# The last stores of a fused retention and hard-swish kernel: who copies the last quarter, and in how many transfers it leaves

## The chip, the cores and the metric

The kernel runs on one core of a Trainium2 chip. The metric is device time in microseconds (us) of one execution, lower is better. Besides plain timings there is one execution under the hardware profiler; its trace and its page are what this document reads.

## The reference

Per batch and head, `ret = ((q k^T) / sqrt(64) * D) v` with the decay mask `D[i, j] = gamma_h^(i-j)` for `i >= j` and zero above. The heads are laid side by side, so that `x` has 4608 rows (8 batches of 576 positions) and 512 columns. Then comes a feed-forward layer:

```python
h = x @ w_in                               # 512 -> 2048
g = h * np.clip(h + 3.0, 0.0, 6.0) / 6.0
out = g @ w_out                            # 2048 -> 512, float32
```

## The kernel before, in words

**Blocks of tokens.** The 576 positions of a batch are cut into 512 "main" positions and 64 "rest" positions. The feed-forward layer works on blocks of 512 tokens (`NMB` is 9). Block `kb` from 0 to 7 holds the main positions of batch `kb`. Block 8, the last, holds the rests of all eight batches: its 512 tokens are eight groups of 64, and 128 neighbouring tokens of it are the rests of two batches.

**Two products per block.** `gemm1` makes the 2048 hidden values (L554 matmuls, L562 on ScalarE, L563 on VectorE). For blocks 2 to 8, `g2_seven` makes the second product by seven half-size products, in the manner of Strassen, instead of eight (`plan`, L738 to L748). Each entry of `plan` is two units, `u = 0` and `u = 1`, of eight matmuls each (L697); `u` is the half of 128 tokens. The output block of 512 tokens by 512 columns is so made in four quarters C11, C12, C21 and C22 of 256 tokens by 256 columns.

**The last block.** There the accumulator named `x` lies in two separate PSUM tiles, which the profile calls `xo` (`u = 0`) and `xtu` (`u = 1`). The last entry of `plan` finishes C21 in them, and nothing is left to do on TensorE after it. `copy_half(u)` (L726 to L729) runs right behind each unit of that entry: it copies one half, 128 tokens by 256 columns, from PSUM to a tile `osh` and calls `store`.

**Where the stores go.** `store` (L594 to L602) and `store_quarter` (L655 to L666) write to the output in DRAM. For a block of rests the 128 tokens of a tile belong to two batches, so that their rows lie in two places of the output, 576 rows apart. Both functions therefore issue two DMA transfers in the last block, one for the first 64 partitions, on the queue of SyncE (SP), and one for the other 64, on the queue of ScalarE (ACT).

**Order.** The order of the instructions on each engine is the order in which the program issues them. A DMA that is issued from ScalarE takes its place in ScalarE's own instruction order, and ScalarE's next copy stands behind it. At the end of the program SP waits for the semaphores of all DMA queues, one after the other (these waits carry the line of the launch, L1067), and then for the other engines.

Of the kernel before, what the change touches and what calls it, by code (L numbers as in the profile page):

```python
# [17 lines left out]
def kernel(  # L18
# [16 lines left out]
    nc = tc.nc  # L35
    B, H, S, D = q.shape
# [4 lines left out]
    HALF = P // 2  # L41
# [4 lines left out]
    MAIN = MBLK  # L46
# [38 lines left out]
    def bank(shape, dtype, name):  # L85
        return psum.tile(shape, dtype, tag="ph", bufs=4, name=name)
# [504 lines left out]
        for fc in range(2):  # L591
            g1_act(kb, banks[fc], fc)

    def store(kb, mc, cols, src):  # L594
        if kb < B:
            r0 = kb * S + P * mc
            nc.sync.dma_start(out[r0:r0 + P, cols], src)
        else:
            for i in range(2):
                r0 = (2 * mc + i) * S + MAIN  # L600
                queue = nc.scalar if i else nc.sync
                queue.dma_start(out[r0:r0 + HALF, cols], src[i * HALF:i * HALF + HALF])  # L602

    pouts = {}

    def g2(kb, mc, part):
        gt = gts[kb]
        if part == 0:
            pouts[kb, mc] = bank([P, DM], FP32, name=f"pout_{kb}_{mc}")
        pout = pouts[kb, mc]  # L610
        for fc in range(4 * part, 4 * part + 4):
            nc.tensor.matmul(pout, gt[:, fc, P * mc:P * mc + P], wout16[:, fc, :],  # L612
                             start=(fc == 0), stop=(fc == NFC - 1))
        if part == 3:
            osb = work.tile([P, DM], FP32, tag="osb", bufs=4, name=f"osb_{kb}_{mc}")
            nc.scalar.copy(osb, pout)
            store(kb, mc, slice(0, DM), osb)

    KH, TH, NH = NFC // 2, MBLK // 2, DM // 2
# [16 lines left out]
    def token_sums(kb, which, c0=0, c1=KH):  # L636

        gt = gts[kb]

        def a(i, j):  # L640
            return gt[:, KH * j + c0:KH * j + c1, TH * i:TH * i + TH]

        def s(name):
            if (kb, name) not in sums:
                sums[kb, name] = work.tile([P, KH, TH], FP16, tag=f"sum_{name}", bufs=1,
                                           name=f"sum_{name}_{kb}")
            return sums[kb, name]

        x, y, op = {"s1": (lambda: a(1, 0), lambda: a(1, 1), ALU.add),
                    "s2": (lambda: s("s1")[:, c0:c1], lambda: a(0, 0), ALU.subtract),  # L650
                    "s3": (lambda: a(0, 0), lambda: a(1, 0), ALU.subtract),
                    "s4": (lambda: a(0, 1), lambda: s("s2")[:, c0:c1], ALU.subtract)}[which]
        nc.vector.tensor_tensor(out=s(which)[:, c0:c1], in0=x(), in1=y(), op=op)  # L653

    def store_quarter(kb, i, j, src):  # L655

        cols = slice(NH * j, NH * j + NH)
        if kb < B:
            r0 = kb * S + TH * i
            nc.sync.dma_start(out[r0:r0 + TH, cols].rearrange("(u p) n -> p u n", u=2), src)  # L660
        else:
            rest = out.rearrange("(m x s) n -> x s m n", x=2, s=S)
            for x in range(2):
                queue = nc.scalar if x else nc.sync
                queue.dma_start(rest[x, MAIN:S, 2 * i:2 * i + 2, cols],
                                src[x * HALF:x * HALF + HALF])  # L666

    def g2_seven(kb, last=False):

        gt = gts[kb]  # L670

        def w(i, j):
            return wout16[:, KH * i:KH * i + KH, NH * j:NH * j + NH]

        def a(i, j):
            return gt[:, KH * j:KH * j + KH, TH * i:TH * i + TH]

        def s(name):
            return sums[kb, name]

        acc = {}

        def get(name):
            if name not in acc:
                if last and name == "x":
                    acc[name] = [psum.tile([P, NH], FP32, tag=t, name=f"x{t}_{kb}")
                                 for t in ("o", "tu")]
                else:
                    whole = bank([P, 2, NH], FP32, name=f"{name}_{kb}")
                    acc[name] = [whole[:, 0], whole[:, 1]]  # L690
                    wholes[name] = whole
            return acc[name]

        def product(name, u, left, right, first):
            dst = get(name)[u]
            for c in range(KH):
                newest[0] = nc.tensor.matmul(  # L697
                    dst, left()[:, c, P * u:P * u + P], right[:, c, :],
                    start=(first and c == 0 and (u == 0 or name not in wholes)),
                    stop=(c == KH - 1), skip_group_check=True)  # L700

        kept, wholes = {}, {}

        def parts(name, tile):
            if name in wholes:
                return [(wholes[name], tile)]
            return [(acc[name][u], tile[:, u]) for u in range(2)]

        def keep(name):
            kept[name] = work.tile([P, 2, NH], FP32, tag="keep_" + {"m5": "m1"}.get(name, name), bufs=1,  # L710
                                   name=f"keep_{name}_{kb}")
            for src, dst in parts({"m5": "z"}.get(name, "x"), kept[name]):
                nc.scalar.copy(dst, src)

        def total(i, j, name, src):
            osb = work.tile([P, 2, NH], FP32, tag="osb", bufs=4, name=f"osb_{kb}_{i}_{j}")
            for (a0, dst), (_, a1) in zip(parts(src, osb), parts(src, kept[name])):
                nc.vector.tensor_tensor(out=dst, in0=a0, in1=a1, op=ALU.add)
            store_quarter(kb, i, j, osb)

        def copy_total():
            osb = work.tile([P, 2, NH], FP32, tag="osb", bufs=4, name=f"osb_{kb}_1_0")
            nc.scalar.copy(osb, wholes["x"])
            store_quarter(kb, 1, 0, osb)

        def copy_half(u):  # L726
            osb = work.tile([P, NH], FP32, tag="osb", bufs=4, name=f"osh_{kb}_{u}")
            nc.scalar.copy(osb, acc["x"][u])
            store(kb, 2 + u, slice(0, NH), osb)  # L729

        def unit(name, u, left, right, first, then=()):
            def do():
                product(name, u, left, right, first)
                for f in then:
                    f()
            return do

        plan = [  # L738
            ("x", lambda: a(0, 0), w(0, 0), True, [lambda: keep("m1")]),
            ("y", lambda: a(0, 1), w(1, 0), True,  # L740
             [lambda: total(0, 0, "m1", "y"), lambda: token_sums(kb, "s3")]),
            ("x", lambda: s("s2"), wts["t2"], False, [lambda: keep("u2")]),
            ("z", lambda: s("s1"), wts["t1"], True,
             [lambda: keep("m5"), lambda: token_sums(kb, "s4")]),
            ("x", lambda: s("s3"), wts["t3"], False, [lambda: total(1, 1, "m5", "x")]),
            ("z", lambda: s("s4"), w(1, 1), False, [lambda: total(0, 1, "u2", "z")]),
            ("x", lambda: a(1, 1), wts["t4"], False, [] if last else [copy_total]),
        ]  # L748
        units = []
        for n, (name, left, right, first, then) in enumerate(plan):  # L750
            for u in range(2):
                after = then if u else []
                if last and n == len(plan) - 1:
                    after = [lambda u=u: copy_half(u)]
                units.append(unit(name, u, left, right, first, after))
        return units
# [315 lines left out]
```

## Time and profile before

| | us |
|---|---|
| median of 3 runs | 294.95 (294.73 to 295.85) |
| the profiled execution's own time | 295.87 |
| its span, first to last instruction | 294.1 |
| outside the span (295.87 - 294.1) | 1.8 |
| TensorE busy in the span | 282.4 (96%) |
| last matmul of C21's second half ends | 289.05 |

The span is what the trace shows; the run's own time is longer than the span by what lies outside it. The profiled execution took 0.9 us more than the median of the plain runs. Times "at 289.49" in the text are us from the start of the span. In lists of groups or of the timeline, a row gives engine, line, operation, the tile written and the tile read. SPq and ACTq are the sequencers of SyncE and ScalarE issuing DMAs. In the list of DMA queues, q1 is the hardware queue that SP issues to, and q10 the one that ScalarE issues to; of each queue come packets, MB, and the packets' time as a share of that of 16 DMA engines over the stretch.

### The profile page before, as it was taken

The page shows a single profiled execution, that of the slowest core. Times are in us where ns is not written, and L with a number is a line of the kernel's source. Part 1 is how long each engine was busy: PE and PEld are TensorE (multiplying, and loading weights), DVE is VectorE, ACT ScalarE, POOL GpSimd, SP SyncE. Part 2 cuts the span into 40 slices and gives each one's busy share as a digit, 9 for nine tenths or more (in the row PEclk, how much of TensorE's full clock was granted, in tenths as well). Part 3 has the DMA queues.
Part 4 walks back from the last instruction along what each step waited for, and adds up shares of the span by engine and source line. Part 5 has one row for each costly group of instructions (what it writes and reads, how often), then busy time and mean ns, then how long its engine had stood idle before and what let it go on. Part 6 is the DMA issues. An engine that isn't in the chain of part 4 may idle for free.

```text
span 294.1 us, 8348 instructions
## 1 busy us (share of the span) xinstructions
PE 282.4 (96%) x3495; PEld 175.5 (60%) x3495; DVE 227.3 (77%) x377; ACT 167.1 (57%) x297; POOL 107.5 (37%) x134
## 2 busy tenths in 40 slices
PE   5999999999999989999999999999999999999993
PEld 1644445644544668458845884588458745874682
DVE  4768656798758996799879987998799588728960
ACT  5567537784358634774477447744774286337711
POOL 8963568359343323333334333455550000000000
PEclk9799999999999999999999999999999999999998
DMA  9999999999999999999999799999992240120014
GB/s 66 148 193 206 189 165 218 161 135 139 127 211 164 152 104 119 168 135 87 120 150 157 79 125 164 128 92 124 151 149 48 74 109 0 38 79 30 0 39 108
DMA packets 156630, 35.68 MB, mean 121 GB/s; under 512 B 143792, under 2 KB 155568, under 8 KB 156592
## 3 DMA queue, kind: packets, MB, share of 16 engines
q0 software_dynamic: 117264, 18.36, 94.7%
q1 hardware_dynamic: 38736, 16.26, 29.5%
q8 instruction: 27, 0.44, 0.7%
q10 hardware_dynamic: 592, 0.52, 0.6%
q14 instruction: 11, 0.09, 0.1%
HBM read 36.70 MB, written 9.44 MB: 157 GB/s over the span
## 4 chain that ended last, share of the span: by engine, by line
PE 86%; DMA 6%; POOL 4%; issue 1%; DVE 1%; ACT 0%; ACTq 0%; POOLq 0%
PE ph L554 39%; PE x L697 14%; PE z L697 9%; PE pout L612 7%; PE y L697 5%; DMA qk<-qv 3%; DMA win<-in_moe_w_in_dram 3%; POOL qv L103 2%; PE o L458 2%; PE sc L425 2%; PE o L479 1%; POOL kn L103 1%; PE ph L577 1%; PE xtu L697 1%; PE xo L697 1%
## 5 line engine op out<-in xcount | busy, mean ns | idle before, releaser
L554 PE MATMUL ph<-xt,win 128*128 128x512 f16 x560 | 122.5, 379 | 0.1
L562 ACT ACTIVATE u<-ph,cb 128x512 f32<-128x512 f32 x144 | 98.4, 688 | 26.0 <-PE ph L554 25.5
L563 DVE SCALAR_TENSOR_TENSOR gt<-u,ph 128x512 f16<-128x512 f32 x144 | 95.7, 683 | 22.4 <-ACT u L562 20.9
L554 PEld LDWEIGHTS <-win 128*128 128x128 f16 x560 | 54.6, 98 | 64.8 <-DMA win<-in_moe_w_in_dram 0.6
L103 POOL DMA_DIRECT2D qv<-in_v_dram x40 | 33.9, 849 | 39.0 <-PE x L697 16.9
L103 POOL DMA_DIRECT2D kn<-in_k_dram x40 | 34.2, 856 | 37.2 <-PE ph L554 12.7
L697 PEld LDWEIGHTS <-sum_s 128*128 128x128 f16 x448 | 42.6, 98 | 6.8 <-issue 1.5
L103 POOL DMA_DIRECT2D qv<-in_q_dram x40 | 33.8, 845 | 31.1 <-PE z L697 9.9
L697 PEld LDWEIGHTS <-gt 128*128 128x128 f16 x336 | 32.1, 98 | 5.5
L612 PE MATMUL pout<-wout,gt 128*128 128x512 f16 x128 | 29.5, 379 | 0.0
L697 PE MATMUL x<-wsum_t,sum_s 128*128 128x256 f16 x192 | 23.1, 273 | 1.2 <-issue 1.2
L531 ACT CAST tm<-th 128x256 f16<-128x256 f32 x24 | 9.7, 405 | 20.4 <-DVE th L526 20.3
L612 PEld LDWEIGHTS <-gt 128*128 128x128 f16 x128 | 11.9, 98 | 13.0
L431 DVE TENSOR_TENSOR at<-sc,mask 128x1024 f16<-128x1024 f32 x14 | 17.0, 1215 | 1.9 <-PE sc L425 1.9
L653 DVE TENSOR_TENSOR sum_s<-gt 128x1024 f16<-128x1024 f16 (+1 forms) x21 | 18.1, 863 | 0.2
L307 DVE TENSOR_TENSOR qv<-qv,gqv 128x1024 f16<-128x1024 f16 x26 | 17.8, 683 | 0.0
L489 ACT CAST xt<-o 128x512 f16<-128x512 f32 x28 | 15.0, 585 | 4.2 <-PE o L479 4.2
L542 DVE TENSOR_TENSOR ta<-u,th 128x256 f32<-128x256 f32 x24 | 10.2, 424 | 6.2 <-ACT th L529 5.2
L697 PE MATMUL z<-wout,sum_s 128*128 128x256 f16 x112 | 14.5, 274 | 0.0
L697 PE MATMUL y<-wout,gt 128*128 128x256 f16 x112 | 14.3, 274 | 0.0
L697 PE MATMUL z<-wsum_t,sum_s 128*128 128x256 f16 x112 | 13.6, 273 | 0.0
L697 PE MATMUL x<-wsum_t,gt 128*128 128x256 f16 x96 | 11.5, 273 | 0.0
(117 smaller groups left out, 256.4 us busy)
## 6 DMA issues: line engine op xcount, KB each, us to landing
out_dram<-osb SPq DMA_DIRECT2D x32, 256.0 KB, 2.5
kn<-in_k_dram POOLq DMA_DIRECT2D x32, 128.0 KB, 6.0
qv<-in_q_dram POOLq DMA_DIRECT2D x32, 128.0 KB, 6.5
qv<-in_v_dram POOLq DMA_DIRECT2D x32, 128.0 KB, 6.1
wout<-in_moe_w_out_dram POOLq DMA_DIRECT2D x4, 512.0 KB, 15.0
win<-in_moe_w_in_dram POOLq DMA_DIRECT2D x3, 512.0 KB, 11.3
win<-in_moe_w_in_dram POOLq DMA_DIRECT2D x2, 256.0 KB, 6.5
kn<-in_k_dram POOLq DMA_DIRECT2D x8, 64.0 KB, 3.6
```

The costliest lines, as they stand in the source:

```text
L103: loaded[c]["dma"].append(nc.gpsimd.dma_start(dst[p0:p0 + n], src[b, :, s0:s0 + n, :].rearrange("h s d -> s h d")))
L307: scaled = nc.vector.tensor_tensor(out=qv, in0=qv, in1=gqv, op=ALU.mult)
L431: nc.vector.tensor_tensor(out=at.rearrange("t a j p s -> t (a j p) s"), in0=sc.rearrange("t a j p s -> t (a j p) s"), in1=mask64[:, None, ...
L489: nc.scalar.copy(xt_at(cs[0], 0, 2 * P).rearrange("e p (j x s) -> e p j x s", j=2, x=2) [:, :, :, half, :], o[half].rearrange("e j p s -> ...
L531: nc.scalar.copy(tm, ta)
L542: nc.vector.tensor_tensor(out=ta, in0=st[c]["u"][1], in1=st[c]["sum"], op=ALU.add)
L554: newest[0] = nc.tensor.matmul(ph, win16[:, dmc, P * fc:P * fc + P], xt_of(kb)[:, dmc, :], start=(dmc == 0), stop=(dmc == NCC - 1))
L562: nc.scalar.activation(u, ph, ACTF.Relu, bias=cb[:, 0:1], scale=1.0 / 6.0)
L563: nc.vector.scalar_tensor_tensor(out=gts[kb][:, fc, :], in0=u, scalar=1.0, in1=ph, op0=ALU.min, op1=ALU.mult)
L612: nc.tensor.matmul(pout, gt[:, fc, P * mc:P * mc + P], wout16[:, fc, :], start=(fc == 0), stop=(fc == NFC - 1))
L653: nc.vector.tensor_tensor(out=s(which)[:, c0:c1], in0=x(), in1=y(), op=op)
L697: newest[0] = nc.tensor.matmul(dst, left()[:, c, P * u:P * u + P], right[:, c, :], start=(first and c == 0 and (u == 0 or name not in whol ...
```

## The change

In the last block, the first half of C21 is copied by VectorE instead of ScalarE; the second half stays on ScalarE. Each half is then stored by one transfer, whose DRAM side goes over two batches, instead of by two transfers with one batch each. The first half's transfer is issued on SP's queue, the second half's on ScalarE's queue. Nothing else changes; the lines behind `store` move by two.

```diff
-    def store(kb, mc, cols, src):
+    def store(kb, mc, cols, src, queue=nc.sync):
         if kb < B:
             r0 = kb * S + P * mc
             nc.sync.dma_start(out[r0:r0 + P, cols], src)
         else:
-            for i in range(2):
-                r0 = (2 * mc + i) * S + MAIN
-                queue = nc.scalar if i else nc.sync
-                queue.dma_start(out[r0:r0 + HALF, cols], src[i * HALF:i * HALF + HALF])
+            rests = out.rearrange("(m x s) n -> m x s n", x=2, s=S)
+            queue.dma_start(rests[mc, :, MAIN:S, cols], src)
...
         def copy_half(u):
             osb = work.tile([P, NH], FP32, tag="osb", bufs=4, name=f"osh_{kb}_{u}")
-            nc.scalar.copy(osb, acc["x"][u])
-            store(kb, 2 + u, slice(0, NH), osb)
+            if u:
+                nc.scalar.copy(osb, acc["x"][u])
+            else:
+                nc.vector.tensor_copy(osb, acc["x"][u])
+            store(kb, 2 + u, slice(0, NH), osb, nc.scalar if u else nc.sync)
```

Seen as the transfer carries it, outermost count first, the DRAM side of a store of this kind was 64 rows of 256 columns, and is now 2 batches of 64 rows of 256 columns. The SBUF side was 64 partitions of 256 columns, and is now 128 partitions of 256 columns.

## The prediction, made blind

> **What bounds the kernel now.** The page comes first: TensorE is busy 96% of the span, and the chain that ended last is 86% TensorE. The change leaves every matmul where it is, so only what follows the last matmul can move. The chain of waits, in its last stretch:
>
> ```profile
> 288.17 0.89 PE xtu L697 x8
> 289.06 0.03 issue
> 289.09 0.38 ACT osh L728
> 289.47 0.02 issue
> 289.49 0.52 ACTq L602
> 290.02 0.04 issue
> 290.06 0.04 ACTq L728
> 290.10 0.04 issue
> 290.14 0.37 ACT osh L728
> ```
>
> The reader is to see that after the last matmul ScalarE works alone and in series: copy `xo`, issue a DMA, copy `xtu`, issue a DMA (290.54). Then the timeline, with start and duration:
>
> ```profile
> 287.34 0.69 DVE L718 TENSOR_TENSOR osb<-z,keep_u 128x512 f32<-128x512 f32 x1 [1.32 <-PE z L697]
> 288.06 0.64 ACTq L665 DMA_DIRECT2D out_dram<-osb  x1
> 289.09 0.37 ACT L728 COPY osh<-xo 128x256 f32<-128x256 f32 x1 [4.61 <-PE xtu L697]
> 290.54 0.51 ACTq L602 DMA_DIRECT2D out_dram<-osh  x1
> ```
>
> VectorE is free at 288.03; `xo` is complete at 288.18 (its eight matmuls start at 287.14 and take 1.04); ScalarE copies it only at 289.09. By the list of waits of the DMA queues, the end hangs on the last store:
>
> ```profile
> SPq L1067 <- DMA out_dram<-osh: 1.7, 1, 1.7
> ```
>
> That store (ScalarE's second, issued at 290.54) moves its packets from 291.98 to 292.41 and signals its landing at 292.75. SP has nine waits there, about 0.06 apart once they are free. The second is for this landing (released at 292.77), the ninth stands at 293.20; barriers end the span at 294.09. Of the queues I look at two stretches, first 282.4 to 283.8, one store of 128 rows on each queue, then 290.6 to 292.6, the four stores of 64 rows and two last packets of the store before:
>
> ```profile
> q1 hardware_dynamic: 144, 0.13, 45.9%
> q10 hardware_dynamic: 144, 0.13, 26.9%
> ...
> q1 hardware_dynamic: 160, 0.13, 26.5%
> q10 hardware_dynamic: 162, 0.13, 25.0%
> ```
>
> A store of 128 rows of 1 KB is 144 packets: 128 of data and 16 closing ones of 4 B. A store of 64 rows is 80: 64 and 16. So 16 engines take part in each, with 8 or 4 rows apiece. 26.9% of 16 engines over 1.4 us is 6.0 us, or 46 ns for a data packet. In the packet records the rows of one engine follow each other every 42.5 ns there.
>
> **The change, part by part.**
>
> *Removed.* One ScalarE copy (0.37) and one ScalarE issue (0.52) ahead of the copy of `xtu`: with the gaps, 290.14 - 289.09 = 1.05 us. That copy waits for `xtu` at 289.06, so it starts at 289.09, and its store is issued at 289.49 instead of 290.54.
>
> *Moved to VectorE.* A 128x256 f32 read of PSUM with a second operand takes VectorE 0.42 (`osb<-xo,keep_m`); I take that as the ceiling and ScalarE's 0.37 as near the floor. The copy starts at 288.21 and ends by 288.64. Its added waits are for stores of earlier blocks, landed long before, and nothing is queued behind it on VectorE. SP is still issuing the previous store until 288.65 and has a wait to pass until 288.72. So the copy costs nothing: SP's queue hides it with 0.08 to spare, and `osh` of `xo` is issued at about 288.74 instead of 289.49. 0.1 more in the copy would be 0.1 later for that store alone.
>
> *Four stores become two.* Two issues of about 0.5 go, one on each queue; what an issue of the new shape takes is bounded by 0.33 (128 rows of 2 KB) and 0.75 (the longest one of 64x2 rows). From issue to first packet the rows show 0.82 (128x2) to 1.38 (64x2, idle queues), 1.15 for SP's 64 rows, 1.42 for ScalarE's 64 rows behind SP's.
>
> *How the new store is dealt to the DMA engines.* This decides. Every store in the trace has an outermost count of 64 or 128 on both sides and is dealt in equal shares to 16 engines. The new one has 128 on the SBUF side, but 2 on the DRAM side. No row shows such a transfer. Bounds: 16 engines with 8 rows each as in the rows above, 128 rows in 0.53 to 0.88 us; or, if the cut goes along the outermost count and must fit both sides, two engines with 64 rows each, 64 x 42.5 ns = 2.72 us. I take two: all rows agree that shares are equal and that the outermost loop is what is shared out (a 64x2 store costs 0.60 of issue, a 128x2 one 0.37, though the latter has twice the rows: the work of issuing follows the outer shape, not the bytes). The Trainium skill says so outright ("DMA: Bandwidth & Descriptors", section on why a DMA increments its semaphore by 16): the engine count is the largest up to 16 that divides the slowest dimension of both sides; here that is 2. No run here shows it yet. The same page's rules for kernel authors speak for the other part of the change: transfers to disjoint partition halves share the same engines, so one of 128 partitions should take their place. The trace agrees that they share: the store of either half has 16 closing packets, on either queue. By that rule alone the sum would be the first rival's.
>
> *Do both new stores use the same two engines?* Both queues have identical shapes and feed the same 16 engines, so I take the same pair. Then each of the two carries 128 rows: 128 x 42.5 = 5.44 us. SP's store starts between 289.9 (288.74 + 1.15) and 290.65 (when the previous store on ScalarE's queue is done); in the first case the pair also has that store's 8 rows to move. The ends are 289.9 + 136 x 0.0425 = 295.7 and 290.65 + 5.44 = 296.1; middle 295.9. Landing follows the last packet by 0.34 to 0.6 in the rows; with 0.35, 296.25. Before it was 292.75: **+3.5 us**.
>
> *Waits at the end.* Each DMA takes the next semaphore of a ring of eight; with two DMAs fewer, the last two landings are the eighth and ninth of SP's waits, where now the last one is the second. Those ahead are passed while the data still moves: 293.20 - 292.77 = **-0.43 us** (0.37 if the eighth lands last).
>
> *Sum.* +3.5 - 0.43 = +3.07. The profiled execution would take 295.87 + 3.07 = 298.9; from the median of the runs, 294.95 + 3.07 = **298.0**. With 52 ns per row (the stores of 256 rows need 0.83 us for 16 rows an engine) it is 128 x 9.5 ns = 1.2 more, 299.2. With the 79 ns of the median packet on SP's 128-row stores in the last block it is 4.7 more, 302.7.
>
> **Rivals.**
>
> *The store still spreads over 16 engines* (faster side). Then the change keeps its gains. ScalarE's store is issued at 289.49, has its first packet at 290.64 to 290.91, takes 0.53 to 0.88 and lands 0.34 to 0.6 later: about 291.95, 0.80 earlier than now. With the 0.43 at the end that is -1.23: 293.7, between 293.3 and 294.2. For it: no store in the trace uses fewer than 16 engines. Against it: none had an outer count that 16 does not divide. It decides wherever the engine count does not follow the DRAM side.
>
> *Two engines each, but different pairs.* Then the stores run side by side. The later one moves from 290.64 or 290.91 for 2.72 (3.33 at 52 ns) and lands at 293.7 to 294.6: +0.95 to +1.9, less 0.43, so 295.5 to 296.4. For it: engines could be handed out in turn. Against: with 16 of 16 taken each time the trace never shows a choice.
>
> *Two engines, slower rows.* An engine that serves two rings alone, row after row into DRAM, may not keep 42.5 ns; beyond 52 ns the time is 299.4 to 302.7. For it: SP's 64-partition stores run at 79 ns even when alone (282.5 to 283.2). Against: stores of 256 rows keep 44 ns over 16 rows an engine.
>
> *The copies do not move apart as the program says.* It does do what it says: the order on the engines has the copy of `xo` last on VectorE, one store on each queue, none other. I give this nothing of its own.
>
> **How the numbers follow.** The measurement can tell about 0.5%, 1.47 us, from no change: faster is below 293.48, slower above 296.42. Same pair at 42.5 to 52 ns, 297.4 to 299.4: 0.60. Slower rows: 0.14. All 16 engines: 0.17, of which 0.05 falls below 293.48. Different pairs: 0.09, within 0.5%. So faster 0.05, same 0.12 + 0.09 = 0.21, slower 0.74. The range takes the different pairs, the same pair and most of the slower rows, 0.09 + 0.60 + 0.11 = 0.80: 295.2 to 301.5. The spread over 16 engines lies outside it.
>
> **What would show it.** Right: `xo` copied on VectorE at about 288.2, SP's `osh` issue near 288.74, ScalarE's at 289.49; from 290.7 to 295.9 DMA engines busy at about 2 of 16, near 1 digit in tenths instead of 5 to 7, some 48 GB/s; and fewer closing packets. With 2 of them per store, q1 goes from 38736 packets to 38736 - 160 + 130 = 38706 and q10 from 592 to 562; with 16 it would be 38720 and 576. Landing of both stores near 296. Wrong: 144 packets per store within 0.9 us and an end near 292.9 (span). Rows every 42.5 ns but in two overlapping bundles that end by 293.6 would mean separate pairs.

## The result, and the profile after

The changed kernel takes 299.6 us (median of 5 runs, 299.09 to 300.0) against 294.95 for the kernel before (5 runs): the ratio is 1.0151, 95% interval 1.0129 to 1.0174. It is slower by 4.65 us. Forecast were 298.0, within 295.2 to 301.5: the side, the mechanism and the range held, the size was 1.6 us short.

The profiled execution's span is 297.8, its own time 299.6. In different executions the same work ahead of the last matmul ends up to 3 us apart (here 0.87 earlier than before: 288.18 against 289.05). So I read every profile from the end of the last matmul on: before, 5.05 us follow it to the end of the span; after, 9.60. The difference, 4.55, accounts for the 4.65 between the medians but for 0.1.

The list of DMA queues on the page after has the packets that two engines per store predict. Here are its lines from the page before, and behind the dots those from the page after:

```profile
q1 hardware_dynamic: 38736, 16.26, 29.5%
q10 hardware_dynamic: 592, 0.52, 0.6%
...
q1 hardware_dynamic: 38706, 16.26, 27.8%
q10 hardware_dynamic: 562, 0.52, 0.5%
```

The timeline of the last stretch (start, duration, engine, line, operation):

```profile
287.14 1.04 PE L695 MATMUL xtu<-wsum_t,gt 128*128 128x256 f16 x8
287.34 0.42 DVE L729 COPY osh<-xo 128x256 f32<-128x256 f32 x1 [0.18 <-PE xo L695]
287.87 0.62 SPq L600 DMA_DIRECT2D out_dram<-osh  x1
288.23 0.37 ACT L727 COPY osh<-xtu 128x256 f32<-128x256 f32 x1 [4.62 <-PE xtu L695]
288.63 1.07 ACTq L600 DMA_DIRECT2D out_dram<-osh  x1
```

The copies and the issues went as the change meant: the second half is issued 0.46 us after the last matmul instead of 1.49. Then nothing but DMA is left, and SP waits for it. Its list of waits from 284 on, where before there was one wait of 1.7 us for `osh`:

```profile
SPq L1068 <- DMA out_dram<-osh: 6.1, 2, 4.0
```

What moves meanwhile is seen in the queues from 293.5 to 294.4, with the DMA engines' busy tenths in 40 slices and the rate below:

```profile
DMA  2020202021111111120202020211111120202020
GB/s 91 0 91 0 91 0 91 0 91 46 46 46 46 46 46 46 46 91 0 91 0 91 0 91 0 91 46 46 46 46 46 46 91 0 91 0 91 0 91 0
...
q10 hardware_dynamic: 31, 0.03, 9.9%
q1 hardware_dynamic: 11, 0.01, 3.5%
```

42 rows of 1 KB in 0.9 us is 48 GB/s: two engines, a row every 42.4 ns each. Both queues appear in the same stretch, and no slice has more than 2 tenths of 16 engines. The packet records say the same. They do not name the DMA engine, so I take rows that follow each other in even steps as those of one engine. While one queue has an engine for itself its rows start 42.4 ns apart; where SP's and ScalarE's store meet on an engine, each queue's rows start 85 ns apart. It is one pair of engines for both stores.

### The profile page after: what moved, and what is told of

It reads as the page before. It is cut to its first block, busy times and chain, and to the rows that moved or that the text cites. A ratio compares the mean times of both kernels' runs of the same rounds, so it can differ in the third digit from the quotient of the medians.

```text
span 297.8 us, 8345 instructions
## 1 busy us (share of the span) xinstructions
PE 282.1 (95%) x3495; PEld 175.5 (59%) x3495; DVE 227.8 (76%) x378; ACT 166.6 (56%) x296; POOL 107.5 (36%) x134
## 4 chain that ended last, share of the span: by engine, by line
PE 88%; POOL 4%; DMA 3%; issue 1%; DVE 0%; ACT 0%; POOLq 0%
PE ph L554 39%; PE x L695 14%; PE pout L610 9%; PE z L695 9%; PE y L695 4%; DMA win<-in_moe_w_in_dram 3%; PE o L458 2%; POOL qv L103 2%; PE sc L425 2%; PE o L479 1%; PE u L510 1%; POOL kn L103 1%; PE ph L577 1%; PE xtu L695 1%; PE xo L695 1%
## 5 line engine op out<-in xcount | busy, mean ns | idle before, releaser
L695 PE MATMUL x<-wout,gt 128*128 128x256 f16 x96 | 11.5, 273 | 0.0
```

The costliest lines, as they stand in the source:

```text
L695: newest[0] = nc.tensor.matmul(dst, left()[:, c, P * u:P * u + P], right[:, c, :], start=(first and c == 0 and (u == 0 or name not in whol ...
```

## Experiments

Theory A: a store is dealt to as many DMA engines as fit the outermost count of its DRAM side, here two; both stores get the same two, and the time is their rows one after the other. The table has all kernels; the one that stores both halves together was timed twice. The last two columns are worked out from the profiles, as us from the end of the last matmul to the last landing of a store and to the end of the span.

| kernel | median | before, same chip | ratio (95%) | landing | end |
|---|---|---|---|---|---|
| before | 294.95 | | | 3.71 | 5.05 |
| changed | 299.6 | 294.95 | 1.0151 (1.0129 to 1.0174) | 8.69 | 9.60 |
| copies apart only | 294.53 | 294.92 | 0.9994 (0.9975 to 1.0014) | 3.48 | 4.82 |
| merging only | 299.39 | 294.92 | 1.0147 (1.0114 to 1.0181) | 8.65 | 9.57 |
| second half merged | 297.95 | 294.92 | 1.0096 (1.0069 to 1.0124) | 6.52 | 7.86 |
| first half merged | 297.98 | 295.15 | 1.0097 (1.0073 to 1.0122) | 6.26 | 7.60 |
| both merged, on SP | 299.72 | 294.92 | 1.0152 (1.0123 to 1.018) | 8.69 | 9.60 |
| rows 2 x 32 | 300.38 | 295.25 | 1.0169 (1.0149 to 1.019) | 8.84 | 10.18 |
| rows 4 x 16 | 297.79 | 295.25 | 1.0077 (1.0054 to 1.01) | 5.54 | 6.88 |
| rows 8 x 8 | 296.6 | 295.15 | 1.0054 (1.0028 to 1.0079) | 4.89 | 6.24 |
| rows 16 x 4 | 295.31 | 295.25 | 1.001 (0.9987 to 1.0034) | 3.78 | 5.11 |
| halves stored together, first time | 294.57 | 295.25 | 0.9978 (0.9955 to 1.0) | 3.26 | 4.24 |
| halves stored together, again | 294.2 | 295.15 | 0.9973 (0.9958 to 0.9988) | 3.25 | 4.23 |
| first half on SP | 294.82 | 295.15 | 0.9998 (0.998 to 1.0017) | 3.47 | 4.76 |

**Copies apart only.** The edit to the kernel before:

```diff
-            nc.scalar.copy(osb, acc["x"][u])
+            if u:
+                nc.scalar.copy(osb, acc["x"][u])
+            else:
+                nc.vector.tensor_copy(osb, acc["x"][u])
```

> The copies as in the changed kernel (VectorE the first half, ScalarE the second), the four stores of 64 rows as before. Theory A (the loss lies in the deal of the store to two DMA engines, the copies apart are a gain): the second half's stores are issued some 0.85 us sooner; the four stores stand closer behind each other in the queues, so the end moves by -0.2 to -0.85 us: 294.1 to 294.75. Rival B (VectorE's copy or the new order of the issues costs time by itself): 294.95 or more. By A 38736 packets on SP's queue and 592 on ScalarE's, as before.

The ratio cannot be told from 1; the stretch at the end is 0.23 shorter, the least that A gave. That VectorE's copy costs time, as rival B would have it, is not seen at the end, though the ratio alone could not rule it out. Half of the 0.85 goes to a new wait: ScalarE's issue for the first half stands ahead of its copy of the second, which starts 0.67 after the last matmul (287.77), and the last issue comes 1.06 after it, 0.43 sooner than before. In ScalarE's timeline:

```profile
286.79 0.63 ACTq L665 DMA_DIRECT2D out_dram<-osb  x1
287.81 0.51 ACTq L602 DMA_DIRECT2D out_dram<-osh  x1
288.44 0.37 ACT L729 COPY osh<-xtu 128x256 f32<-128x256 f32 x1 [5.23 <-PE xtu L697]
```

**Merging only.** The edit to the changed kernel:

```diff
-            if u:
-                nc.scalar.copy(osb, acc["x"][u])
-            else:
-                nc.vector.tensor_copy(osb, acc["x"][u])
+            nc.scalar.copy(osb, acc["x"][u])
```

> Both copies on ScalarE as before, each half stored by one transfer as in the changed kernel. Theory A: 128 rows on each of two engines as in the changed kernel, 38706 and 562 packets; SP's store is issued up to 0.75 us later, so 299.6 to 300.4. Rival B (the copy on VectorE was part of the loss): below 299.3.

The time lies between A's stretch and B's bound. The stretch to the end, 9.57 against 9.60, says that who copies makes no difference once the stores are merged: the first store is issued 0.74 later and its packets start 0.18 later, but the pair of engines is through at the same time. All of the loss comes with the merging.

**Only one half merged.** In the two kernels `store` merges one half alone; the other is stored in two transfers of 64 rows:

```diff
-            queue.dma_start(rests[mc, :, MAIN:S, cols], src)
+            if mc % 2:                      # the other kernel: mc % 2 == 0
+                queue.dma_start(rests[mc, :, MAIN:S, cols], src)
+            else:
+                for i in range(2):          # both on SP; the other kernel: SP and ScalarE
+                    queue.dma_start(rests[mc, i, MAIN:S, cols], src[i * HALF:i * HALF + HALF])
```

> Copies as in the changed kernel; the first half is stored in two transfers of 64 rows, both on SP's queue, only the second half in one transfer on ScalarE's queue. Theory A (two engines, 42.5 ns a row): 64 rows on each of two engines, 2.72 us, the first at about 1.4 to 1.9 us after the last matmul; end 0.9 to 1.6 us later than before, 295.8 to 296.5. Rival C (a store of this shape on ScalarE's queue starts its packets 4 us after its issue, as in the changed kernel, whatever else the two engines do): about 3.4 us later, 298.3.

> Copies as in the changed kernel; the first half is stored in one transfer on SP's queue, the second half in two transfers of 64 rows, one on each queue. Theory A with a slow start: 64 rows on each of two engines; the changed kernel's first store began to move 1.5 us after the last matmul, the slower of the two engines only from 2.2 and with 0.75 of slow rows, so it is through at 2.2 + 0.75 + 2.6 and lands at 5.9; end 1.5 to 2.0 us later than before, 296.4 to 296.9, less than the 2.8 us that the merged second store alone cost. Rival (each merged store costs the same, half of the changed kernel's loss): 2.3 us, 297.2.

The second half alone costs 2.81 at the end, between A and C. Its packets do not start 4 us after the issue but 2.16, so C falls; they start 2.62 after the last matmul instead of 1.4 to 1.9. ScalarE's issue took 1.21, 0.69 more than the 0.52 of before; without that, by my estimate, they would have started at 1.93. Then one of the two engines has three packets of 261 ns before it runs at 42.4. In the queues from 290.55 to 294.2 the slices at the left are thin, the steady digit 1 (two engines) comes only a third of the way on, and at the right one engine is done before the other; all 130 packets of the store lie in the stretch:

```profile
DMA  1020020020001111111111111111110000000000
...
q10 hardware_dynamic: 130, 0.13, 11.3%
q1 hardware_dynamic: 3, 0.00, 0.1%
```

That is 3.56 us for 64 rows per engine, where 2.72 was reckoned. The first half alone costs 2.55, where I expected 1.5 to 2.0. Its own store lands at 6.07 (expected 5.9), but the other half's rows on 16 engines stand behind it on the two busy ones and land at 6.26, in a place that SP's waits come to early. So a store on few engines also delays a store on all of them (the last landing before was at 3.71). The rival's 2.3 is nearer.

**Both merged stores on SP's queue.** The edit to the changed kernel:

```diff
-            store(kb, 2 + u, slice(0, NH), osb, nc.scalar if u else nc.sync)
+            store(kb, 2 + u, slice(0, NH), osb, nc.sync)
```

> The changed kernel with both transfers on SP's queue. Theory A alone (128 rows on each of two engines, with a slow start whichever queue they come from): 299.3 to 299.9. Theory D (the 1.5 us by which the changed kernel exceeds the forecast come from two queues serving the same two engines at once): up to 1.3 us less, about 298.3, and no packets of 150 to 300 ns at the start.

Theory D falls: 9.60 to the end, as in the changed kernel, and the slow packets at the start are there too (207 and 316 ns on one engine, 228, 247 and 242 on the other). SP's issues took 0.63 and 0.53, not ScalarE's 1.07, and that changed nothing, because the pair was busy throughout.

**The outermost count alone.** In the kernel before, the DRAM side of the four stores is listed in another order, with A of 2, 4, 8 and 16:

```diff
-                queue.dma_start(out[r0:r0 + HALF, cols], src[i * HALF:i * HALF + HALF])
+                rows_out = out[r0:r0 + HALF, cols].rearrange("(b a) n -> a b n", a=A)
+                queue.dma_start(rows_out, src[i * HALF:i * HALF + HALF])
```

With 2, 4, 8 and 16 alike, C21's rows in that block land in other places of the output than the reference has them; these four kernels serve the timing alone.

> The kernel before with one thing changed: in each of the four stores of 64 rows in the last block, the DRAM side lists its rows as 2 x 32 (every other row) instead of 64; nothing is merged, both copies stay on ScalarE. C21's rows in the last block land in another order. Theory A (the outermost count on the DRAM side sets the number of DMA engines): 2 engines with 4 x 32 = 128 rows each; from 1.6 us after the last matmul, 0.75 for the slow first rows, 5.43 for the rows and 0.33 to land; with SP's waits behind that, 299.3; 38708 and 564 packets. Rival E (the loss of the changed kernel comes from the 128 partitions or the two distant batches of its merged transfer, or from the order of the work): as before, 294.9, and 38736 and 592 packets.

> As the kernel with rows as 2 x 32, but as 4 x 16. Theory A: 4 engines with 64 rows each, 2.71 us instead of 5.43: 296.6; 38712 and 568 packets. Rival E: 294.9.

> As the kernel with rows as 2 x 32, but as 8 x 8. Theory A: 8 engines with 32 rows each, 1.36 us of rows; the stretch from the last matmul to the end was 10.2 with 2 engines, 6.9 with 4 and 5.1 with 16; between the last two here, 5.2 to 5.7: 295.0 to 295.6; 38720 and 576 packets.

> As the kernel with rows as 2 x 32, but as 16 x 4: the control for the row order and the extra dimension. Theory A: 16 engines, as before within 0.3: 294.6 to 295.3; 38736 and 592 packets. If the extra dimension or the order costs by itself: later than that.

Rival E falls. Bytes, partitions, queues and the number of issues are the same; only the count moves, and with it the time: 5.11, 6.24, 6.88 and 10.18 us to the end for 16, 8, 4 and 2. The control with 16 cannot be told from the kernel before (5.05 to the end, ratio 1.001), so the order of the rows and the extra dimension cost nothing that is seen here. The packets follow to the last one; q1 and q10 for 2, 4, 8 and 16, each from its own page:

```profile
q1 hardware_dynamic: 38708, 16.26, 28.5%
q10 hardware_dynamic: 564, 0.52, 0.5%
```

```profile
q1 hardware_dynamic: 38712, 16.26, 28.7%
q10 hardware_dynamic: 568, 0.52, 0.5%
```

```profile
q1 hardware_dynamic: 38720, 16.26, 28.5%
q10 hardware_dynamic: 576, 0.52, 0.5%
```

```profile
q1 hardware_dynamic: 38736, 16.26, 27.7%
q10 hardware_dynamic: 592, 0.52, 0.5%
```

This is the rule of the Trainium skill ("DMA: Bandwidth & Descriptors", why a DMA increments its semaphore by 16), and these four runs agree with it at every count. With 2, 4 and 8 the stretch to the end came out longer than A's sums (9.4, 6.7 and at most 5.7). The timeline with 8 shows one part:

```profile
288.07 1.41 ACTq L603 DMA_DIRECT2D out_dram<-osh  x1
289.60 0.37 ACT L729 COPY osh<-xtu 128x256 f32<-128x256 f32 x1 [1.56 <-DMA out_dram<-osh]
```

ScalarE's first issue takes 1.41 instead of 0.52, and its copy of the second half, next in line, starts 1.96 after the last matmul instead of 1.09. With 16 it starts at 1.16, with 4 and 2 at 1.93 and 1.89. Against the control with 16, then, the second half is 0.80 late with 8 engines before any row of it moves, and the end is 1.13 late. Most of what 8 engines cost seems to go with the long issue; with 2 engines the end is 5.07 late, far more than that issue explains.

**Merging that keeps the count.** Both halves are copied into one tile, VectorE and ScalarE one each, and stored by `store_quarter`: two transfers by batch parity, 64 rows outermost, two halves next. The edit to the kernel before:

```diff
-            osb = work.tile([P, NH], FP32, tag="osb", bufs=4, name=f"osh_{kb}_{u}")
-            nc.scalar.copy(osb, acc["x"][u])
-            store(kb, 2 + u, slice(0, NH), osb)
+            if not u:
+                kept["c21"] = work.tile([P, 2, NH], FP32, tag="osb", bufs=4, name=f"osh_{kb}")
+                nc.vector.tensor_copy(kept["c21"][:, 0], acc["x"][0])
+            else:
+                nc.scalar.copy(kept["c21"][:, 1], acc["x"][1])
+                store_quarter(kb, 1, 0, kept["c21"])
```

> Copies apart as in the changed kernel, into one tile for both halves, which is then stored in two transfers by batch parity (partitions 0 to 63 on SP's queue, 64 to 127 on ScalarE's), 64 rows outermost and the two halves next, as the block's other quarters are. Theory A: two transfers instead of four, each on 16 engines; issued 0.43 us after the last matmul, landing near +3.4 to 3.7 and with SP's last waits already passed: 0.4 to 0.9 us faster than before, 294.0 to 294.5. Rival F (waiting for both halves costs what the merging saves): 294.9 or more.

> The kernel that copies on two engines and stores both halves together by batch parity, once more for a narrower interval: 0.4 to 0.9 us faster than before (ratio 0.997 to 0.9985); from the last matmul to the end 4.2 us instead of 5.05.

The first time it took 294.57 against 295.25 (ratio 0.9978, 0.9955 to 1.0), the second time 294.2 against 295.15 (0.9973, 0.9958 to 0.9988): 0.3% faster than the kernel before, and the second interval excludes 1. Rival F falls. This is the best version here. In the timeline of the second run the last issues come 0.43 after the last matmul (287.89), and nothing stands ahead of the copy:

```profile
287.92 0.37 ACT L731 COPY osh<-xtu 128x256 f32<-128x256 f32 x1 [4.60 <-PE xtu L697]
288.32 0.59 SPq L665 DMA_DIRECT2D out_dram<-osh  x1
288.32 0.63 ACTq L665 DMA_DIRECT2D out_dram<-osh  x1
```

**First half on SP.** The edit to the kernel with copies apart only:

```diff
-                queue = nc.scalar if i else nc.sync
+                queue = nc.scalar if i and mc % 2 else nc.sync
```

> Copies apart, four stores of 64 rows on 16 engines each, both of the first half on SP's queue so that ScalarE's copy of the second half waits for no issue; the second half's on SP and ScalarE. From the kernel with copies apart alone (end 4.8 us after the last matmul) the copy of the second half starts 0.6 us sooner: 4.2 to 4.5, so 294.1 to 294.4 or 0.5 to 0.8 us faster than before. Rival (SP's three issues in a row hold the last store back): 4.8 or more.

The copy does start 0.61 sooner (0.05 after the last matmul), and almost nothing comes of it: 4.76 to the end against 4.82, next to the rival's 4.8. SP's third issue begins at 288.91, 1.0 after the last matmul, as late as ScalarE's last issue without the move (1.07), and the last store lands at 3.47, as it did there at 3.48.

## Why the prediction was right, and where it was short

**The part that was removed and moved: right.** VectorE's copy took 0.42 and was hidden behind SP's queue; SP's issue came 0.30 before the end of the last matmul (forecast 0.31), ScalarE's 0.46 after it (forecast 0.44). That issue then took 1.07, outside the bounds of 0.33 to 0.75; no cost of it is seen, for with both stores on SP, issued in 0.63 and 0.53, the end is the same 9.60.

**Two engines, and the same two: right.** Shown by the packet counts, by the interleaving at 85 ns, and by the kernels that change the count alone. The 42.5 ns per row held as well (42.4), and so the rival of other pairs and the one of rows that are slow throughout fall. One argument for the deal did not carry: the issue times do not follow the outer count. In the kernel before, 64 rows took 0.49, 64x2 rows 0.60 and 128x2 rows 0.37 on SP, and the new store with an outer count of 2 took 0.62. The rival with 16 engines would have been worth what it said in kind: the kernel that merges and keeps the count gains 0.82 at the end (5.05 to 4.23) where 1.23 was reckoned.

**The waits at the end: right.** From the last landing to the end of the span it was 1.34 before and 0.91 after, the 0.43 of the forecast.

**The term that was short: when the pair starts, and its first rows.** The sum let the pair work without a gap from about 1.4 us after the last matmul and be through at 6.85 (295.9 in the time of before). It was through at 8.36, which is 1.5 later, the whole miss against +3.07. Its first packet came at 1.47, in time (though 1.77 after the issue, more than the 1.38 of the rows); but the slower engine's only at 2.21, 0.8 late, and three of its first rows took 227, 252 and 252 ns instead of 46. With the pauses behind them their starts stand 286, 311 and 248 ns from the next instead of 42, which is 0.7 more. Together that is the 1.5. The landing after that was 0.32 (0.35 reckoned).

The sum also left out a packet that is no store's. In the queues from 289.4 to 292.6 it has a line of its own:

```profile
q14 instruction: 1, 0.01, 0.6%
```

This instruction packet of 8 KB runs from 1.91 to 2.22 after the last matmul, for 309 ns. The slower engine's first row starts 3 ns before that packet's end, as closely as one engine's rows follow each other (46 ns long, 42.4 apart). The same 3 ns are there with both stores on SP, with the first half merged and with rows 2 x 32; with merging only, the row starts 27 ns after the end. As far as the times can tell, the packet held that engine, and 0.31 of the 0.8 went to it. Ahead of it ScalarE's previous store was still moving: its last row ends at 1.91, where before it ended at 1.61.

**What the numbers would have needed.** 299.6 lies where I put "slower rows", at 0.14, and not in the likeliest case's own stretch of 297.4 to 299.4. The rows of before gave the rate in full flow on 16 engines; none could show a start on two.

Left open: why the first rows on few engines are slow. Of packets over 140 ns after the last matmul, the 8 KB instruction packets aside, there are none with 16 and with 8 engines, 4 with 4 engines and 9 with 2 (four kernels that differ in the count alone); they come with both queues in use and with SP's alone. Which step makes them was not tried.

## What to carry to other kernels

A transfer that is merged from two should keep a large outermost count on both sides, the DRAM side too (here 16 cost nothing that is seen, 8, 4 and 2 did): merge along an inner dimension. Count the small closing packets in the list of queues to see how many engines a transfer got, and read the tail from the last matmul on, since what lies ahead of it varied by up to 3 us from one execution to another. Where few engines do serve a transfer, rows per engine times the row time is a lower bound: here the start added half as much again to the loss that it gave.

## What the runs showed of the hardware that was not expected

- On ScalarE's queue the first store on fewer than 16 engines took long to issue: 1.07, 1.14, 1.21, 1.32, 1.34 and 1.41 us in six kernels. The second took 0.54 to 0.64 where there was one, and SP's issues of the same shapes 0.53 to 0.70.
- In the kernel before, ScalarE's issue of a 64x2 store ended at 288.70, but its copy of `xo` started only at 289.09, though `xo` had come at 288.19. The trace puts this down to `xtu`, which ended at 289.06. But the same pause of 0.39 stands in the kernel with copies apart only, where what is held up is an issue that waits for VectorE alone, ready 0.06 before the pause began. What makes it stays open.
- Two stores issued at the same moment on the two queues do not start together: ScalarE's first packet follows SP's by 0.67 to 0.72 for 64x2 rows (0.54 and 0.58 for the last pair of the two runs that store both halves together) and by 0.27 to 0.30 for 64, on 16 engines.
